# Attention with the product with v turned round, and ten chunks of inner features instead of nine in the first feed-forward phase

## The chip, the core and the metric

One core of a Trainium2 chip runs the whole program. The metric is the device time of one execution in microseconds (us); for the kernel before it is the median of three runs. An engine is named as the profile names it: PE is TensorE (matmuls), PEld its weight loads, DVE is VectorE, ACT is ScalarE, POOL is GpSimd, and SP is the queue that issues all DMAs here.

## What is computed

Causal attention with decay over 4 batches of 8 heads (576 positions, 64 features a head), a feed-forward layer of 2304 tokens (512 to 2048 to 512, leaky ReLU), and a second one (512 to 1024 to 512) with a softmax gate and a layer norm. Cut to what matters:

```python
scores = scale * np.matmul(q, k.transpose(0, 1, 3, 2))
scores = np.where(causal, -1000000000.0, scores + decay)
scores = scores - np.max(scores, axis=-1, keepdims=True)
attn = np.exp(scores)
attn = attn / (np.sum(attn, axis=-1, keepdims=True) + 1e-09)
return np.matmul(attn, v)                       # _attn_ref
h = x @ w_in; g = np.maximum(0.01 * h, h); return g @ w_out   # _moe_ref
solu = h * softmax(h); return layernorm(solu, g_ln) @ w_out   # _moe2_ref, shortened
```

## The kernel before

**How the order comes about.** The kernel doesn't write its instructions in the order in which they run. `body` declares operations (`P.op`) with an engine, an estimated duration, a priority and the buffers they write and read; `Plan.run` then plays them through a model of the engines and writes each instruction at the moment the model gives it an engine. A buffer is a tile of a tag (`P.tag("ps_v", ...)`); an operation whose tag has no free tile waits in the model, and a tile can be handed on to another tag when its own has no further use (`heirs`). On the chip each engine then runs its list strictly in that order. Attention has lower priority numbers (127 to about 500) than the feed-forward layer (from 1000), so feed-forward matmuls fill what attention leaves of PE.

**Attention** goes by pairs of heads: 16 pairs, four to a batch (`pair`, L765 on). The first four pairs are done in two parts, query blocks 0 and 1 (128 rows each) first and blocks 2, 3 and 4 later; the other twelve in one. For a unit of query blocks `scores` puts q times k into a PSUM bank `ps_s` (four banks), DVE adds the mask and takes the row's minimum (L693), and `softmax` goes on: ACT takes the exponential and sums the row (`accum_out`, L643), the sum is guarded and scaled (L652 to L657) and inverted (L661), ACT copies the row times the inverse to f16 as the high half (L424, tile `hl`), and DVE writes the rest as the low half (L435). A DMA turns `hl` into `pt` (L467), so that keys lie on the partitions. `pv` then multiplies: the stationary operand is a 128x128 block of v, 64 columns of high halves beside 64 of low halves (`vl`), and the moving one is `pt`, 128 queries wide:

```python
for k in range(2):
    mm(ps.t[:, 128 * i:128 * i + 128], vl(p, hd, j), pts[i][0].t[:, pts[i][1] + k * (i + 1) + j, :],
       j == 0 and k == 0, j == i and k == 1)
```

The result stands with features on the partitions, the high and the low sum in different halves, and `evac` adds the two and rescales (ACT L725, then DVE L728) into `xr`, which goes to memory. `pv4` does the same for block 4, whose 64 rows of both heads share one softmax; its moving operand is 64 wide. All products use the one PSUM bank `ps_v`.

**The feed-forward layer** goes in two phases over nine blocks of 256 tokens. In the first (`ffn_a`) `FA` = 9 of the 16 chunks of 128 inner features are computed for every block, and the partial output is stored; in the second (`ffn_b`) the other seven, then the second layer (`layer2`, `layer2_out`). A block of the first phase needs all four pairs of its batch in memory (`load_x`, `deps`): blocks 0 and 1 need batch 0, blocks 2 and 3 batch 1, blocks 4 and 5 batch 2, and blocks 6 to 8 batch 3. A chunk of one block takes 24 matmuls with 256 columns, so nine chunks take 216. The first phase starts when its weights have been unpacked from the staging tiles `wst` (`main`, L1024).

Of the kernel before, what the change touches and what calls it, by code (L numbers as in the profile page):

```python
# [24 lines left out]
FA = 9  # L25
PT = 4
NVT = 4
# [3 lines left out]
WI0 = 9  # L31
# [326 lines left out]
def body(tc, kqa, kq, vt, f, wa, w2i, w2o, gln, out):  # L358
# [16 lines left out]
    P.tag("raw", tiles(base, "raw", 2, [128, KQ], F32))  # L375
    P.tag("wk", tiles(base, "wk", 2, [128, 512], I32))
# [20 lines left out]
    mask = ap.tile([128, 512], BF16, name="mask")  # L397
    mask4 = ap.tile([128, S], BF16, name="mask4")
# [74 lines left out]
    def setup():  # L473
# [120 lines left out]
    def prep_v(p, prio):  # L594
# [6 lines left out]
        half = lambda l: v.t[:, :, :, l].rearrange("p j h d -> p (j h) d")  # L601

        def sums():
            with nc.allow_low_precision(reason="only the exponent of the largest sum is used"):
                nc.scalar.activation(v.t.rearrange("p j h l d -> p (j h l d)")[:, 0:640], R(), AF.Abs, accum_out=va.t)
# [6 lines left out]
            v.t.rearrange("p j h l d -> p (j h l d)")[:, 0:256].bitcast(F32), ps.t[:, 0:128], mask[:, 0:128], -1.0, -(2.0 ** -97),  # L612
            ALU.add, ALU.min, col(1)), prio + PV, w=[(vs, 1)], rw=[v], r=[ps])
# [3 lines left out]
        P.op(DVE, 70, lambda: nc.vector.tensor_scalar(u.t.bitcast(I32), e(), float(29 << 23), None, op0=ALU.subtract), prio + PV + 1,  # L617
# [18 lines left out]
    def softmax(parts, prio):  # L636


        sts, n, nb = parts[0][1], 0, len(parts)
        hl, pt = P.buf("hl"), P.buf("pt")  # L640
        one = parts[0][2] == parts[-1][2]
        for k, (view, _, j, W, pieces, ps) in enumerate(parts):
            P.op(ACT, act(W, 1, True) + 93, lambda view=view, j=j, k=k: nc.scalar.activation(  # L643
                view(), view(), AF.Exp, bias=sts.t[:, j:j + 1], scale=-1.0, accum_out=sts.t[:, 3 + k:4 + k]), prio,
                w=[(sts, 2)], rw=[ps], r=[(sts, j)])

        ns = 1 if one else nb
        total, scale = lambda: sts.t[:, 3:3 + ns], lambda: sts.t[:, 6:6 + ns]

        def guard(e):  # L650
            if one and nb == 2:
                nc.vector.scalar_tensor_tensor(scale(), total(), 1.0e-9, sts.t[:, 4:5], op0=ALU.add, op1=ALU.add)  # L652
                nc.vector.tensor_scalar(scale(), scale(), PS, None, op0=ALU.mult)
            elif e == ACT:
                nc.scalar.activation(scale(), total(), CP, scale=PS, bias=1.0e-9 * PS)
            else:
                (nc.vector if e == DVE else nc.gpsimd).tensor_scalar(scale(), total(), 1.0e-9, PS, op0=ALU.add, op1=ALU.mult)  # L657

        engs = (DVE,) if one and nb == 2 else REC_ENGS
        flex(engs, [{ACT: 100.0, DVE: 70.0 * nb, POOL: 165.0}[e] for e in engs], guard, prio, w=[(sts, 3)], r=[(sts, 2)])  # L660
        P.op(DVE, 75, lambda: nc.vector.reciprocal(sts.t[:, 9:9 + ns], scale()), prio, w=[(sts, 4)], r=[(sts, 3)])  # L661
        for view, _, j, W, pieces, ps in parts:
            rs = lambda j=j: sts.t[:, 9 + j:10 + j]
            for ho, lo, so, w in pieces:
                copy_f(lambda ho=ho, w=w: hl.t[:, ho:ho + w], lambda so=so, w=w, view=view: view()[:, so:so + w], w, prio,
                       engs=HI_ENGS, scale=rs, psum=True, w=[(hl, ho)], r=[ps, (sts, 4)])
            for ho, lo, so, w in pieces:
                sub_f(lambda lo=lo, w=w: hl.t[:, lo:lo + w], lambda so=so, w=w, view=view: view()[:, so:so + w],
                      lambda ho=ho, w=w: hl.t[:, ho:ho + w], w, prio, engs=(DVE,), scale=rs,
                      w=[(hl, lo)], r=[ps, (sts, 4), (hl, ho)])  # L670
                n += 2 * w
        turn(lambda: pt.t[:, 0:n // 128], lambda: hl.t[:, 0:n], n, prio - 500, w=[pt], r=[hl])
        return pt

    def scores(p, unit, hd, prio, full):

        sts, parts, n, at = P.buf("st"), [], 0, 0
        for j, i in enumerate(unit):
            W = 128 * (i + 1)
            joint = i < 2 and len(unit) > 1  # L680
            if i == 1 and joint:
                at = 128
            else:
                ps, at = P.buf("ps_s"), 0
            view = lambda at=at, W=W, ps=ps: ps.t[:, at:at + W]
# [3 lines left out]
                **({"rw": [ps]} if at else {"w": [ps]}))  # L689
            parts.append([view, sts, j, W, [(n, n + W, 0, W)], key, i])  # L690
            n += 2 * W
        for view, _, j, W, _, key, i in parts:
            P.op(DVE, dve(W) + 130, lambda i=i, j=j, view=view: nc.vector.tensor_tensor_reduce(  # L693
                view(), view(), mask[:, 384 - 128 * i:512], -0.125, 3.0e38, ALU.add, ALU.min, sts.t[:, j:j + 1]),
                prio, w=[(sts, j)], rw=[key])
        parts = [x[:6] for x in parts]
        pt = softmax(parts, prio)
        return {i: (pt, x[4][0][0] // 128) for i, x in zip(unit, parts)}

    def scores4(p, prio, full):  # L700
# [4 lines left out]
        for ps, k0, k1, init in ((pa, 0, 512, 3.0e38), (pb, 512, S, None)):  # L705
            def pe(ps=ps, k0=k0, k1=k1, Q=QK[p]):
                for hd in range(2):
# [5 lines left out]
                ps.t[:, 0:n], ps.t[:, 0:n], mask4[:, k0:k1], -0.125, sts.t[:, 1:2] if init is None else init,  # L713
# [412 lines left out]
```

## Time and profile before

| what | value |
|---|---|
| median of 3 runs | 850.28 us (850.12 to 850.7) |
| the profiled execution, its own time | 849.04 us |
| its span, first to last instruction | 847.2 us |
| PE busy | 777.7 us, 92% of the span |
| PEld busy | 707.1 us, 83% |
| DVE busy | 523.0 us, 62% |
| ACT busy | 488.8 us, 58% |
| POOL busy | 364.5 us, 43% |

The span and the time of one execution differ by 1.84 us that lie outside the first and last instruction. Busy shares are means over stages that differ: attention runs until 368 us, the first phase goes on alone until 464 us, and the second phase and second layer take the rest. A matmul's own duration holds its way through the array as well; what one costs in a row of its kind is the distance from one start to the next.

### The profile page before, as it was taken

The page shows a single profiled execution, that of the slowest core. Times are in us where ns is not written, and L with a number is a line of the kernel's source. Part 1 is how long each engine was busy: PE and PEld are TensorE (multiplying, and loading weights), DVE is VectorE, ACT ScalarE, POOL GpSimd, SP SyncE. Part 2 cuts the span into 40 slices and gives each one's busy share as a digit, 9 for nine tenths or more (in the row PEclk, how much of TensorE's full clock was granted, in tenths as well). Part 3 has the DMA queues.
Part 4 walks back from the last instruction along what each step waited for, and adds up shares of the span by engine and source line. Part 5 has one row for each costly group of instructions (what it writes and reads, how often), then busy time and mean ns, then how long its engine had stood idle before and what let it go on. Part 6 is the DMA issues. An engine that isn't in the chain of part 4 may idle for free.

```text
span 847.2 us, 15672 instructions
## 1 busy us (share of the span) xinstructions
PE 777.7 (92%) x5648; PEld 707.1 (83%) x5648; DVE 523.0 (62%) x1301; ACT 488.8 (58%) x1210; POOL 364.5 (43%) x433
## 2 busy tenths in 40 slices
PE   2477799987899999999999999999999999999997
PEld 2345689975798889999999998899889988998985
DVE  7899888887878788736544755334342434243641
ACT  5799798977988889736644533332433243324321
POOL 7888757546756474026311323322332233223321
PEclk9999899995899999999999999999999999999999
DMA  9799778787868786755554513321314131312113
GB/s 285 199 231 226 178 142 183 129 185 156 184 137 179 126 197 115 147 165 187 168 175 157 190 26 87 71 68 26 87 38 101 26 88 38 87 26 63 26 42 95
DMA packets 179757, 106.66 MB, mean 126 GB/s; under 512 B 146608, under 2 KB 162496, under 8 KB 179680
## 3 DMA queue, kind: packets, MB, share of 16 engines
q1 hardware_dynamic: 179680, 105.67, 52.3%
q8 instruction: 44, 0.72, 0.4%
q14 instruction: 33, 0.27, 0.1%
HBM read 55.72 MB, written 14.78 MB: 83 GB/s over the span
## 4 chain that ended last, share of the span: by engine, by line
PE 58%; DVE 4%; DMA 3%; ACT 3%; issue 1%; POOL 1%; DVEq 0%; SPq 0%; ACTq 0%; POOLq 0%
PE ps_f L470 36%; PE ph L470 11%; PE py L470 8%; DMA pt<-hl 2%; PE ps_s L470 1%; PE ps_v L470 1%; DMA tr<-hl 1%; ACT hl L424 1%; DVE hl L435 1%; DVE st L657 0%; ACT ps_s L643 0%; DVE g L841 0%; DVE raw L952 0%; DVE ps_s L693 0%; DVE s L944 0%
## 5 line engine op out<-in xcount | busy, mean ns | idle before, releaser
L470 PE MATMUL ps_f<-x,wi 128*128 128x256 f32 x972 | 129.6, 288 | 0.8 <-DVE g L841 0.8
L470 PEld LDWEIGHTS ps_f<-x,wi 128*128 128x128 f32 x972 | 123.6, 193 | 2.0 <-DVE g L841 1.2
L470 PE MATMUL ps_f<-g,wo 128*128 128x256 f32 x972 | 124.2, 283 | 1.2 <-DVE g L841 1.2
L470 PEld LDWEIGHTS ps_f<-g,wo 128*128 128x128 f32 x972 | 119.5, 188 | 1.8 <-DVE g L841 1.5
L470 PE MATMUL ps_s<-kq 128*128 128x512 f32 (+4 forms) x352 | 95.4, 396 | 25.8 <-DVE hl L435 22.4
L470 PE MATMUL ps_f<-x,wib 128*128 128x256 f32 x756 | 98.3, 281 | 0.7 <-DVE g L841 0.4
L470 PEld LDWEIGHTS ps_s<-kq 128*128 128x128 f32 x352 | 65.9, 226 | 39.2 <-DVE hl L435 22.2
L470 PE MATMUL ph<-wi,g 128*128 128x512 f32 x408 | 98.3, 396 | 0.0
L839 ACT ACTIVATE g<-ps_f 128x256 fp32r<-128x256 f32 x144 | 55.2, 383 | 71.9 <-PE ps_f L470 70.8
L470 PEld LDWEIGHTS ps_f<-x,wib 128*128 128x128 f32 x756 | 92.8, 188 | 1.8 <-DVE g L841 1.7
L470 PEld LDWEIGHTS ph<-wi,g 128*128 128x128 f32 x408 | 76.0, 188 | 17.6
L439 POOL TENSOR_TENSOR kq<-raw,kq 64x576 fp32r<-64x576 f32 (+2 forms) x55 | 82.6, 1502 | 14.6 <-ACT kq L424 9.2
L435 DVE SCALAR_TENSOR_TENSOR hl<-ps_s,st,hl 128x512 f16<-128x512 f32 (+4 forms) x160 | 82.2, 538 | 9.1 <-ACT hl L424 7.3
L643 ACT ACTIVATE ps_s<-ps_s,st 128x512 f32<-128x512 f32 (+4 forms) x160 | 78.8, 493 | 13.0 <-DVE st L693 7.7
L841 DVE TENSOR_TENSOR g<-ps_f,g 128x256 fp32r<-128x256 f32 x144 | 60.2, 420 | 41.0 <-ACT ps_f L840 39.3
L470 PE MATMUL ps_f<-wo,x 128*128 128x512 f32 x348 | 83.9, 396 | 0.0
L424 ACT ACTIVATE hl<-ps_s,st 128x512 f16<-128x512 f32 (+4 forms) x146 | 73.0, 538 | 12.3 <-issue 3.2
L470 PEld LDWEIGHTS ps_f<-wo,x 128*128 128x128 f32 x348 | 64.7, 188 | 14.9
L470 PE MATMUL ps_v<-pt,VT 128*128 128x128 f16 (+1 forms) x928 | 65.4, 234 | 12.7 <-DVE xr L728 4.3
L470 PE MATMUL py<-g,wob 128*128 128x256 f32 x567 | 76.6, 279 | 0.0
L470 PEld LDWEIGHTS <-VT 128*128 128x128 f16 x928 | 56.2, 110 | 22.8 <-issue 13.2
L470 PEld LDWEIGHTS py<-g,wob 128*128 128x128 f32 x567 | 72.4, 188 | 1.9
(152 smaller groups left out, 1198.5 us busy)
## 6 DMA issues: line engine op xcount, KB each, us to landing
wst<-wa SPq DMA_DIRECT2D x17, 512.0 KB
raw<-wa SPq DMA_DIRECT2D x15, 512.0 KB
raw<-kq SPq DMA_DIRECT2D x12, 608.0 KB
xw<-xs_d SPq DMA_DIRECT2D x24, 256.0 KB
yp_d<-yo SPq DMA_DIRECT2D x36, 128.0 KB
yw<-yp_d SPq DMA_DIRECT2D x18, 256.0 KB
out<-ot SPq DMA_DIRECT2D x18, 256.0 KB
vr<-vt SPq DMA_DIRECT2D x13, 320.0 KB
```

Source lines behind the costliest of these rows:

```text
L424: nc.scalar.activation(o, i, CP, scale=1.0 if scale is None else scale)
L435: nc.vector.scalar_tensor_tensor(o, a, scale, b, op0=ALU.mult, op1=ALU.subtract)
L439: (nc.vector if eng == DVE else nc.gpsimd).tensor_tensor(o, a, b, op=ALU.subtract)
L470: nc.tensor.matmul(o, lhsT=l, rhs=r, start=start, stop=stop)
L643: P.op(ACT, act(W, 1, True) + 93, lambda view=view, j=j, k=k: nc.scalar.activation(view(), view(), AF.Exp, bias=sts.t[:, j:j + 1], scale=- ...
L839: P.op(ACT, act(n, 0, True), lambda: nc.scalar.activation(g.t[:, 0, 0:n], h(), AF.Prelu, scale=WSC, alpha=0.01), eprio, w=[(g, 0)], r=[ps])
L841: P.op(DVE, dve(n) + 60, lambda: nc.vector.tensor_tensor(g.t[:, 1, 0:n], h(), g.t[:, 0, 0:n].bitcast(F32), op=ALU.subtract), eprio, w=[(g, ...
```

## The change

The product with v is turned round. `pt` is now the stationary operand (128 keys by 128 queries) and v the moving one: 65 columns of high halves, the 65th being ones, and 64 of low halves. So a query has a row, its 64 features beside each other, and the 65th column holds the sum of its weights. For one block of keys there are four matmuls (`pv_mms`) where there were two. `softmax` no longer sums, guards, inverts or rescales: it takes the exponential and splits it with a constant factor, and blocks 0 and 1 of a unit are split in one go. After the product three DVE operations (`divide`) guard the sums, invert them and scale the rows into `xn` (or `xn4`); PE turns these 128x128 blocks in its transpose mode (`across`, and the end of `pv4`) into `ps_v`, and one copy brings them to `xr`.

`FA` goes from 9 to 10, so a block of the first phase has 240 matmuls and one of the second 144 instead of 168. For the space, tiles `sd` are handed on as `xw` and `yo`, `x` has seven tiles instead of eight, and `yo` three instead of four. Cut to its core:

```diff
-FA = 9
+FA = 10
+NXN = 1
-WI0 = 9
+WI0 = 10
...
+        for v in P.tags["VT"].free:
+            nc.gpsimd.memset(v[:, 640:1300].rearrange("p (a d) -> p a d", d=66)[:, :, 64:65], 1.0)
...
-                view(), view(), AF.Exp, bias=sts.t[:, j:j + 1], scale=-1.0, accum_out=sts.t[:, 3 + k:4 + k]), prio,
+                view(), view(), AF.Exp, bias=sts.t[:, j:j + 1], scale=-1.0), prio, rw=[ps], r=[(sts, j)])
...
-        P.op(DVE, 75, lambda: nc.vector.reciprocal(sts.t[:, 9:9 + ns], scale()), prio, w=[(sts, 4)], r=[(sts, 3)])
...
+        for view, at, W, ps in groups:
+            copy_f(lambda at=at, W=W: hl.t[:, at:at + W], view, W, prio, engs=HI_ENGS, scale=lambda: 1.0 / PS, psum=True, w=[(hl, at)], r=ps)
+            sub_f(lambda at=at, W=W: hl.t[:, at + W:at + 2 * W], view, lambda at=at, W=W: hl.t[:, at:at + W], W, prio, engs=(DVE,),
+                  scale=lambda: 1.0 / PS, w=[(hl, at + W)], r=ps + [(hl, at)])
...
-    def evac(p, hd, ps, xr, c0, c1, dst0, prio):
...
+    def pv_mms(o, pair, v, first, last):
+        h, l = pair
+        vlo, vhi = v
+        mm(o, h, vhi, first, False)
+        mm(o[:, 0:64], h, vlo, False, False)
+        if l is not None:
+            mm(o[:, 0:64], l, vlo, False, False)
+            mm(o, l, vhi, False, last)
...
+    def divide(p, ps, rs, xn, dst, rows, nb, prio, key):
+        o = lambda a, b: ps.t[0:rows, 0:65 * nb].rearrange("p (n d) -> p n d", d=65)[:, :, a:b]
+        P.op(DVE, 70, lambda: nc.vector.tensor_scalar(rs.t[0:rows, 0:nb].unsqueeze(2), o(64, 65), 1.0e-9 / PS, None, op0=ALU.add), prio,
+             w=[(rs, 0)], r=[ps])
+        P.op(DVE, 75, lambda: nc.vector.reciprocal(rs.t[0:rows, 4:4 + nb], rs.t[0:rows, 0:nb]), prio, w=[(rs, 1)], r=[(rs, 0)])
+        P.op(DVE, dve(64 * nb) + 60, lambda: nc.vector.scalar_tensor_tensor(
+            dst(), o(0, 64), U[p].t[0:rows], rs.t[0:rows, 4:4 + nb].unsqueeze(2).to_broadcast([rows, nb, 64]),
+            op0=ALU.mult, op1=ALU.mult), prio, w=[(xn, key)], r=[ps, (rs, 1), U[p]])
...
+                    pv_mms(o, (pt.t[:, j, c], pt.t[:, 4 + j, c]), vl(p, hd, j), j == 0, False)
...
+        P.op(PE, 40.0, lambda: nc.tensor.transpose(ps.t[:, 256:320], xn.t.rearrange("p h d -> p (h d)"), ident[0:64, 0:64].bitcast(F32)), prio,
+             rw=[ps], r=[xn])
+        copy_f(lambda: xr.t[:, 512:S], lambda: ps.t[:, 256:320], 64, prio, engs=HI_ENGS, psum=True, w=[(xr, 1)], r=[ps])
+
+    def across(p, xn, blocks, xr, prio):
...
+            for i in blocks:
+                nc.tensor.transpose(ps.t[:, at(i)], xn.t[:, i], ident.bitcast(F32))
...
+        copy_f(lambda: xr.t[:, a:b], lambda: ps.t[:, a:b], b - a, prio, engs=HI_ENGS, psum=True, w=[(xr, 0)], r=[ps])
...
-        heirs("x", *(["x2"] * 4 + ["ln"] * 4))
+        heirs("x", *(["x2"] * 3 + ["ln"] * 4))
```

**What the order makes of it.** On PE, in the products of one head's query blocks with v. Before, each 128-column matmul has a weight load of v (`VT`) ahead of it:

```order
L470 LDWEIGHTS VT_108
L470 MATMUL ps_v_164<-pt_131,VT_108 128x128
L470 LDWEIGHTS VT_108
L470 MATMUL ps_v_164<-pt_131,VT_108 128x128
L470 LDWEIGHTS VT_108
L470 MATMUL ps_v_164<-pt_131,VT_108 128x128
```

Now each matmul of 65 or 64 columns has a load of `pt`, and there are twice as many of both:

```order
L477 LDWEIGHTS pt_135
L477 MATMUL ps_v_171<-VT_110,pt_135 128x65
L477 LDWEIGHTS pt_135
L477 MATMUL ps_v_171<-VT_110,pt_135 128x64
L477 LDWEIGHTS pt_135
L477 MATMUL ps_v_171<-VT_110,pt_135 128x64
L477 LDWEIGHTS pt_135
L477 MATMUL ps_v_171<-VT_110,pt_135 128x65
```

On DVE, after the product of block 4 in the changed kernel: the guard (L742) and the inverse (L744) of the sums, and a few rows later the scaling (L745) into `xn4`, between mask rows (`ISA`, L684), feed-forward rows (L858) and low halves (L442) of other units:

```order
L742 TENSOR_SCALAR rs_115<-ps_v_171 64x2
L744 RECIPROCAL rs_115<-rs_115 64x2
L684 ISA ps_s_168,st_126<-ps_s_168,mask 128x512
L684 ISA st_126 128x1
L858 TENSOR_TENSOR g_944<-ps_f_163,g_944 128x256
L745 SCALAR_TENSOR_TENSOR xn_118<-ps_v_171,u_119,rs_115 64x128
L442 SCALAR_TENSOR_TENSOR hl_133<-ps_s_169,hl_133 128x512
```

These rows take the place of the two halves of `evac`, and PE's turn of `xn4` waits for the sixth of them. On PE again, where blocks 0 and 1 of the first phase are used up and block 2 may begin. Before, these are the last rows of a stretch of 165 matmuls of attention without a feed-forward row in it, in which six groups of products with v lie:

```order
L470 MATMUL ps_s_161<-kq_0_140 128x512
L470 MATMUL ps_s_161<-kq_1_141 128x512
L470 MATMUL ps_s_162<-kq_0_144 128x64
L470 MATMUL ps_s_162<-kq_1_145 128x64
L470 MATMUL ps_s_162<-kq_0_140 128x64
L470 MATMUL ps_s_162<-kq_1_141 128x64
L470 MATMUL ps_f_154<-x_854,wi_63 128x256 x3
```

Now the stretch has 140 matmuls, with three groups of products in it, and ends with a turn:

```order
L477 MATMUL ps_s_169<-kq_0_147 128x384
L477 MATMUL ps_s_169<-kq_1_148 128x384
L477 MATMUL ps_s_170<-kq_0_149 128x512
L477 MATMUL ps_s_170<-kq_1_150 128x512
L775 MATMUL ps_v_171<-ident,xn_114 128x128 x4
L477 MATMUL ps_f_163<-x_936,wi_63 128x256 x3
```

Ahead of PE's last product with v stood 1188 matmuls of the first phase, and now 1020 stand ahead of its last turn.

## Rows read from the trace of the kernel before

**Rows 1.** The page's 40 slices: PE's busy tenths, and its granted clock.
```profile
PE   2477799987899999999999999999999999999997
...
PEclk9999899995899999999999999999999999999999
```
**Rows 2.** Busy time by stage: stretch and its length, each engine's busy us, clock, DMA share.
```profile
core 0: us, PE busy (x) PEld busy (x) DVE busy (x) ACT busy (x) POOL busy (x), PEclk, DMA share, GB/s
...
28.00:98.00 70.00, 45.67 (x246) 33.68 (x245) 63.76 (x178) 58.92 (x139) 56.44 (x62) 0.99 0.88 213
98.00:183.00 85.00, 82.52 (x744) 79.12 (x744) 71.14 (x223) 76.39 (x207) 52.06 (x50) 0.96 0.78 159
183.00:219.00 36.00, 24.52 (x168) 20.46 (x168) 29.87 (x91) 26.55 (x71) 21.30 (x22) 0.68 0.79 168
219.00:368.00 149.00, 143.90 (x1342) 137.08 (x1342) 118.32 (x360) 127.69 (x357) 71.39 (x76) 0.98 0.74 148
...
464.00:801.00 337.00, 336.33 (x2167) 303.60 (x2166) 151.60 (x290) 118.38 (x259) 99.55 (x147) 1.00 0.27 66
```
**Rows 3.** Groups of PE's matmuls by line between 98 and 183 us.
```profile
L470 PE MATMUL ps_f<-x,wi 128*128 128x256 f32 x216 | 31.1, 298 | 0.7 <-DVE g L841 0.7
L470 PE MATMUL ps_f<-g,wo 128*128 128x256 f32 x215 | 28.1, 284 | 1.2 <-DVE g L841 1.2
```
**Rows 4.** PE in order of time around the gap: start, us, instructions, idle before.
```profile
183.19 1.29 PE L470 MATMUL ps_v<-pt,VT 128*128 128x128 f16 x20
...
219.05 2.91 PE L470 MATMUL ps_f<-x,wi 128*128 128x256 f32 x12
```
**Rows 5.** Who waited for whom on PE: 28 to 98, 183 to 219, the whole run.
```profile
PE ps_s L470 <- DVE hl L435: 12.8, 9, 3.9
...
PE ps_s L470 <- DVE hl L435: 8.6, 3, 3.8
...
PE ps_v L470 <- DVE xr L728: 4.3, 4, 1.8
```
**Rows 6.** PE in order of time near attention's end.
```profile
361.80 0.70 PE L470 MATMUL ps_v<-pt,VT 128*128 128x64 f16 x18
362.34 4.56 PE L470 MATMUL ps_f<-x,wi 128*128 128x256 f32 x36
366.74 1.29 PE L470 MATMUL ps_v<-pt,VT 128*128 128x128 f16 x20
367.84 2.40 PE L470 MATMUL ps_f<-g,wo 128*128 128x256 f32 x18
```
**Rows 7.** PE in order of time, small f32 matmuls of the scores, and what follows them.
```profile
234.59 0.42 PE L470 MATMUL ps_s<-kq 128*128 128x128 f32 x2
234.84 1.65 PE L470 MATMUL ps_f<-x,wi 128*128 128x256 f32 x12
...
242.78 0.53 PE L470 MATMUL ps_s<-kq 128*128 128x64 f32 x4
243.14 1.68 PE L470 MATMUL ps_f<-g,wo 128*128 128x256 f32 x12
```
**Rows 8.** The chain that ended last: PE runs in the first phase and in the second.
```profile
368.03 13.02 PE ps_f L470 x108
...
464.95 1.76 PE ps_f L470 x15
```
**Rows 9.** The page's groups by line of what the softmax and `evac` lose.
```profile
L728 DVE SCALAR_TENSOR_TENSOR xr<-ps_v,u,xr 64x64 f32<-64x64 f32 (+2 forms) x72 | 34.7, 482 | 8.3 <-ACT xr L725 7.0
L725 ACT ACTIVATE xr<-ps_v,u 64x64 f32<-64x64 f32 (+2 forms) x72 | 33.8, 470 | 10.5 <-PE ps_v L470 6.4 <-DVE xr L728 2.7
L643 ACT ACTIVATION_READ_ACCUMULATOR ps_s<-ps_s,st 128x1 f32 x160 | 32.4, 203 | 0.2
L661 DVE RECIPROCAL st<-st 128x1 f32<-128x1 f32 (+2 forms) x88 | 14.2, 163 | 10.5 <-POOL st L657 6.7 <-ACT st L655 2.4
L652 DVE SCALAR_TENSOR_TENSOR st<-st 128x1 f32<-128x1 f32 x16 | 10.3, 642 | 0.5 <-ACT ps_s L643 0.3
```

More of the change, by code (lines that the diff above doesn't have):

```diff
@@ L375, in body @@
     P.tag("raw", tiles(base, "raw", 2, [128, KQ], F32))
+    P.tag("sd", tiles(base, "sd", 3, [128, S + 2], F32))
     P.tag("wk", tiles(base, "wk", 2, [128, 512], I32))
@@ L396, in body @@
     P.tag("va", tiles(ap, "va", 2, [128, 1], F32R))
[L397 to L398 removed]
+    mask = ap.tile([128, 640], BF16, name="mask")
+    mask4 = ap.tile([128, 64], BF16, name="mask4")
     zcol = ap.tile([32, 1], F32, name="zcol")
@@ L634, in qk_mm, with softmax @@
         mm(o, b[0:68, c0:c0 + 128], b[0:68, k0:k1], False, last)
-    def softmax(parts, prio):
-        sts, n, nb = parts[0][1], 0, len(parts)
+    def softmax(sts, parts, groups, prio):
         hl, pt = P.buf("hl"), P.buf("pt")
-        one = parts[0][2] == parts[-1][2]
-        for k, (view, _, j, W, pieces, ps) in enumerate(parts):
-            P.op(ACT, act(W, 1, True) + 93, lambda view=view, j=j, k=k: nc.scalar.activation(
-                view(), view(), AF.Exp, bias=sts.t[:, j:j + 1], scale=-1.0, accum_out=sts.t[:, 3 + k:4 + k]), prio,
[L645 to L660, printed above, removed]
-        P.op(DVE, 75, lambda: nc.vector.reciprocal(sts.t[:, 9:9 + ns], scale()), prio, w=[(sts, 4)], r=[(sts, 3)])
[L662 to L671, printed above, removed]
@@ L675, in scores @@
     def scores(p, unit, hd, prio, full):
-        sts, parts, n, at = P.buf("st"), [], 0, 0
+        sts, parts, groups, chunk, at = P.buf("st"), [], [], {}, 0
         for j, i in enumerate(unit):
@@ new lines, in pv_mms, with pv, pe @@
+    def pv_mms(o, pair, v, first, last):
[6 more added lines that the diff above has]
+            mm(o, l, vhi, False, last)
+    def pv(p, hd, pts, xn, prio):
+        ps, rs, blocks = P.buf("ps_v"), P.buf("rs"), sorted(pts)
+        bufs = {id(x[0]): x[0] for x in pts.values()}
+        nb, b0 = len(blocks), blocks[0]
+        def pe():
+            for n, i in enumerate(blocks):
+                pt, h, l = pts[i]
+                for j in range(i + 1):
+                    pv_mms(ps.t[:, 65 * n:65 * n + 65], (pt.t[:, h + j], pt.t[:, l + j]), vl(p, hd, j), j == 0, j == i)
+        P.op(PE, sum(4 * (i + 1) * mmh(65) for i in blocks), pe, prio, w=[ps], r=[VT[p]] + list(bufs.values()))
+        divide(p, ps, rs, xn, lambda: xn.t[:, b0 % 4:b0 % 4 + nb, 64 * hd:64 * hd + 64], 128, nb, prio, hd)
@@ L740, in pe @@
+    def across(p, xn, blocks, xr, prio):
+        ps = P.buf("ps_v")
+        at = lambda i: slice(128 * i, 128 * i + 128)
         def pe():
             for i in blocks:
-                for j in range(i + 1):
-                    for k in range(2):
-                        mm(ps.t[:, 128 * i:128 * i + 128], vl(p, hd, j), pts[i][0].t[:, pts[i][1] + k * (i + 1) + j, :],
-                           j == 0 and k == 0, j == i and k == 1)
-        P.op(PE, sum(2 * (i + 1) * mmh(128) for i in blocks), pe, prio, w=[ps], r=[VT[p]] + list(bufs.values()))
@@ L782, in pair @@
                 k += 1
+        across(p, xn, [i for i in blocks if i < 4], xr, prio + AV)
         c0, c1 = 128 * blocks[0], min(S, 128 * blocks[-1] + 128)
```

109 lines of the change are left out of this document (53 added, 56 removed).

## The prediction

> **What bounds the kernel now.** Read the slices of the page first [rows 1]: PE is nearly full from the middle on, and not in the first four slices or around the ninth and tenth, where its granted clock falls too. Then the table by stage [rows 2], which says why. From 464 to 801 us PE is busy 336.33 of 337 us; whatever the change adds to PE there, or takes, is paid in full. From 219 to 368 us, with attention and the first phase side by side, it is busy 143.90 of 149 us, and from 98 to 183 us 82.52 of 85 us. Two stretches are not PE's. From 28 to 98 us no feed-forward block is ready and attention runs alone: DVE is busy 63.76 of 70 us, the DMA engines 88%, PE 45.67 us. And from 183 to 219 us PE has nothing but attention again: it is busy 24.52 of 36 us at a mean granted clock of 0.68.
>
> The reason for that gap is the input of the first phase. Between 98 and 183 us PE ran 216 and 215 matmuls of it [rows 3], two blocks of 216 but for a record that is missing; the third needs batch 1. The time line shows no matmul of the first phase from 183.19 to 219.05 us [rows 4], and the waits in it are for a bank of scores that DVE has yet to free, 8.6 us in 3 waits, as from 28 to 98 us, 12.8 us in 9 [rows 5]. So the time is PE's work, plus what PE loses in these two stretches and at both ends. The change adds to the first and takes from the second.
>
> **What PE gets more of.** Prices are distances from one start to the next. Twenty products with 128 columns take from 366.74 to 367.84 us, 55 ns each; eighteen with 64 columns from 361.80 to 362.34 us, 30 ns each [rows 6]. Each has a weight load of its own, so the loads don't set the pace at either width.
>
> - Heads' blocks: 640 products of 55 ns (35.2 us) become 1280 of 64 or 65 columns at 30 ns (38.4 us): 3.2 us more.
> - Block 4: 288 of 30 ns (8.6 us) become 576 (17.3 us): 8.6 us more. Here the number doubles and the width stays.
> - Turns: 64 of 128 columns and 16 of 64, in f32. No row has one. The low end is the 55 ns of an f16 product of 128 columns [rows 6]; the high end twice the 125 ns at which two f32 matmuls of 128 columns stand (234.59 to 234.84 us), if a turn should need two passes. Four f32 matmuls of 64 columns in a row take 90 ns each (242.78 to 243.14 us) [rows 7]. Turns come in fours too, so I take 90 ns: 7.2 us (4.4 to 20).
> - The tenth chunk: 216 matmuls go from the second phase (15 in 1.76 us, 117.3 ns) to the first (108 in 13.02 us, 120.6 ns) [rows 8]: 0.7 us more.
>
> Together 19.7 us. What of it runs ahead of the first feed-forward row, where PE waits anyway, is free: by the changed order that is 280 products and 12 turns, 9.5 us, where the same units took 104 x 55 and 36 x 30 ns, 6.8 us. That leaves 19.7 - 2.7 = **17.0 us on the path**.
>
> The rows at 55 and 30 ns hold a load for every matmul. The Trainium skill ("TensorE: Matmul & The Clock Gate", Back-to-back issue gap) has a rule that speaks against the change: a stream of load and matmul pairs settles at about 81 ns for 128 columns, set by both. If a pair cost that at any width, 928 more pairs would be an estimated 75 us. The trace doesn't agree: 55 ns at 128 columns and 30 at 64.
>
> **What goes from the other engines.** ACT loses 160 reads of the sum (32.4 us) and 72 rows of `evac` (33.8 us), and gets 36 copies, at the 470 ns of an `evac` row 17 us. DVE loses 34.7, 14.2 and 10.3 us [rows 9] and gets 56 times guard, inverse and scaling; at 163, 163 and 482 ns from the same rows that is at most 45.2 us, so 14 us go at the least, of the 283 us that DVE is busy from 28 to 368 us [rows 2], or 5%. The scaled rows are shorter than most of `evac`'s, so it may be twice that. Where PE is full this hides behind PE and is worth nothing. It counts in the two other stretches:
>
> - **28 to 98 us.** DVE is 91% busy, so 5 to 10% of its work is 3 to 6 us. The DMA engines are 88% busy and have a weight chunk more to bring in here (`WI0` = 10), so 8.4 us is the most. I take 6 us.
> - **183 to 219 us.** Two blocks are now 480 matmuls of the first phase instead of 432, so they last 48 x 120.6 ns = 5.8 us longer, while attention, with a shorter chain in each unit, comes further beside them. The changed order has three groups of products in the gap where there were six. Half of 36 us is 18 us; the attention that has left it, half of 24.52 us at the lower level of 1.2 GHz, costs about 6 us elsewhere at 2.4 GHz: 12 us gained. In what is left a unit no longer waits for the sum's read (203 ns), the guard and the inverse (163 ns) [rows 9]; over three groups with some four units I take 2 us. Together 14 us.
>
> The handed-on tiles (`xw`, `yo`, seven `x`) I cost at nothing: the y matmuls of a block last 120 x 120.6 ns = 14.5 us, in which one more `x` tile has to be split. Where that cover fails, PE would wait at each block's start.
>
> **Sum.** 849.04 (the profiled execution) + 17.0 - 6 - 14 = 846.0 us, 3.0 us less. The median of the runs, 850.28 us, stands 1.24 us above that execution, so I forecast **847.2 us**, with a range of its own from 842 to 853. A measurement of this kernel can tell about 0.2%, or 1.7 us.
>
> **The rivals.**
>
> *The gap closes (faster).* If attention is held up by its chain more than I take, it reaches batch 1's end before the two blocks run out. For it: every wait in the gap is for a bank that the chain frees [rows 5], and the change takes pieces from just that chain. Against it: the order still has 140 matmuls there. The gap's full loss is 36 - 12.3 = 23.7 us, 9.7 more than I took, and the first stage may give its 8.4 us: 847.2 - 12.1 = 835 us.
>
> *Narrow weights (slower).* Block 4's stationary operand is now 64 columns wide, and no row has an f16 load of that width; the eighteen at 30 ns load 128. The nearest slow case is the f32 matmul of 64 columns at 90 ns with a 128-column load of f32 [rows 7], half of which, for half the columns, is 45 ns. Then 504 of the 576 products (72 stand in the first stage) cost 15 ns more each: 7.6 us, **854.8 us**. It decides from 36 ns a product on, where 504 x 6 ns eats the 3.0 us. The Trainium skill ("TensorE: Matmul & The Clock Gate", Weight-path perf modes) says that the fast load is used for 128 weights only, and gives a load of P columns as P / 1.2 ns, an estimated 53 ns here, or 11.6 us more; no row here shows it.
>
> *Turns that wait (slower).* PE stops in its order at a turn until three DVE rows are done, and feed-forward rows queue behind it. There are 36 such steps, 29 of them after the first feed-forward row. For it: PE waited for `evac`'s DVE row 4 times, 1.08 us each [rows 5]. Against it: 4 of 72. If one in three of the 29 waits that long, it is 10.4 us: 857.6 us.
>
> **How the numbers follow.** Forecast 0.40, gap closes 0.25, narrow weights 0.22, turns that wait 0.13. Of my own case half (0.20) ends under 848.6 us, 0.13 within 0.2%, and 0.07 above. So faster is 0.20 + 0.25 = 0.45, the same 0.13, slower 0.07 + 0.22 + 0.13 = 0.42. The range goes from 834, which takes in most of the closed gap, to 863, which takes in both slow rivals with turns at twice my price.
>
> **What would show it.** Right: 1,856 products at about 30 ns where PE runs full; turns near 90 ns; first matmul of the first phase at 90 to 94 us instead of 98; a gap of 14 to 18 us after 480 matmuls of it; attention's last turn about 20 us before 368 us (1020 instead of 1188 feed-forward matmuls stand ahead of it); no new wait of PE for `xn`. Wrong: block 4's products at 40 ns or more; a turn of 200 ns; PE's waits for DVE rows L745 summing to over 5 us; a gap as long as before, or none; or a second phase in which PE is less than 99% busy, for want of an `x` or `yo` tile.

## The result, and the profile after

The changed kernel takes 859.64 us (median of 4 runs, 859.17 to 866.02), the kernel before on the same chip 850.49 us (4 runs, 850.12 to 851.58): a ratio of 1.0123, 95% interval 1.0092 to 1.0153. It is slower, where 847.2 us was forecast. The profiled execution took 859.84 us, with a span of 858.0 us, 10.8 us more than before.

The page of the changed kernel, engines first, then the slices that answer to [rows 1]:

```profile
PE 791.4 (92%) x6656; PEld 720.9 (84%) x6656; DVE 471.9 (55%) x1212; ACT 438.0 (51%) x968; POOL 355.9 (41%) x414
...
PE   1756899999799899999999999999999899999997
...
PEclk9999999999999999999999999999999999999999
```

DVE and ACT got rid of 51 us each, and the dip of the clock in the tenth slice is gone. PE is busy 13.7 us longer. The table by stage, which answers to [rows 2] (PE's idle time is a stretch's length less its busy time):

```profile
core 0: us, PE busy (x) PEld busy (x) DVE busy (x) ACT busy (x) POOL busy (x), PEclk, DMA share, GB/s
0.00:100.36 100.36, 55.80 (x386) 43.30 (x386) 77.14 (x211) 66.81 (x129) 69.58 (x76) 1.00 0.87 223
28.00:100.36 72.36, 47.03 (x361) 36.34 (x359) 59.09 (x157) 50.44 (x99) 49.62 (x42) 1.00 0.85 210
...
211.40:223.90 12.50, 9.48 (x143) 8.39 (x141) 7.63 (x30) 7.81 (x17) 7.83 (x8) 0.86 0.47 113
...
480.00:808.00 328.00, 322.05 (x2061) 288.95 (x2060) 144.67 (x271) 119.45 (x253) 109.93 (x156) 1.00 0.30 76
...
100.36:480.00 379.64, 369.02 (x4008) 353.11 (x4007) 227.41 (x697) 237.79 (x561) 162.89 (x161) 0.99 0.64 148
```

The same stretches of the kernel before, cut at its own first matmul of the first phase and at 50 us ahead of its end:

```profile
0.00:98.08 98.08, 53.84 (x269) 39.82 (x270) 85.72 (x232) 77.82 (x183) 78.86 (x94) 1.00 0.87 228
...
480.00:797.20 317.20, 316.53 (x1997) 283.80 (x1996) 139.20 (x268) 108.72 (x237) 92.49 (x135) 1.00 0.26 62
...
98.08:480.00 381.92, 362.70 (x3179) 347.87 (x3180) 278.53 (x773) 288.40 (x766) 180.31 (x185) 0.96 0.70 161
```

The gap shrank from 35.9 to 12.5 us, more than forecast. The first phase starts at 100.36 us instead of 98.08, in spite of a DVE that is only 82% busy from 28 us on. And from 480 us on PE, which idled 0.67 us, now idles 5.95. What PE did at the lower of its two clock levels is in the stretches with a granted clock of 0.50, of before:

```profile
97.23:104.06 6.83, 6.83 (x29) 6.64 (x30) 5.63 (x17) 5.60 (x14) 6.68 (x7) 0.50 0.71 166
189.39:192.80 3.41, 3.41 (x24) 3.01 (x25) 1.97 (x8) 2.19 (x6) 2.60 (x2) 0.50 1.11 277
196.22:213.29 17.07, 13.78 (x82) 11.53 (x83) 13.66 (x44) 12.66 (x34) 10.49 (x11) 0.50 0.64 142
216.70:223.52 6.82, 6.82 (x37) 6.36 (x38) 4.57 (x16) 6.09 (x19) 5.56 (x8) 0.50 1.02 227
```

and of the changed kernel:

```profile
219.20:222.61 3.41, 3.33 (x43) 3.27 (x43) 0.88 (x5) 0.92 (x4) 0.61 (x1) 0.50 0.32 77
297.71:301.12 3.41, 3.41 (x17) 3.41 (x17) 3.02 (x8) 2.52 (x7) 3.34 (x3) 0.50 0.87 175
```

30.84 us of work at the lower level (1.2 instead of 2.4 GHz) became 6.74 us. What the level costs is seen at the first phase's start in the kernel before, where twelve feed-forward matmuls take 2.71 us, 226 ns each, against the 120.6 ns of [rows 8]:

```profile
98.08 2.91 PE L470 MATMUL ps_f<-x,wi 128*128 128x256 f32 x12
100.79 1.70 PE L470 MATMUL ps_s<-kq 128*128 128x512 f32 x4
```

So about half of the difference, an estimated 12.0 us, is time won between these two executions. It is a loose term: experiment 7, which has the same order on PE, spends 13.7 us at the lower level after the start of its first phase, and among the four runs of the changed kernel the profiled one has the highest mean granted clock (0.996; the others 0.986 to 0.992).

A granted clock of 1.00 isn't always the pace at which PE goes. Ahead of the first phase the page prints 1.00, yet the last 28 products there take 1.57 us in the changed kernel, 56 ns each. Forty in the stretch printed as 0.50 take 2.16 us, 54 ns each:

```profile
96.81 1.75 PE L477 MATMUL ps_v<-VT,pt 128*128 128x65 f16 x28
98.38 2.14 PE L477 MATMUL ps_s<-kq 128*128 128x384 f32 x6
...
219.28 2.35 PE L477 MATMUL ps_v<-VT,pt 128*128 128x65 f16 x40 [1.34 <-ACT xr L431]
221.44 1.59 PE L477 MATMUL ps_s<-kq 128*128 128x384 f32 x4
```

In experiment 8, with the same order on PE up to there, the same 28 take 0.85 us, 30 ns each:

```profile
93.12 1.02 PE L477 MATMUL ps_v<-VT,pt 128*128 128x65 f16 x28
93.97 1.54 PE L477 MATMUL ps_s<-kq 128*128 128x384 f32 x6
```

So a busy microsecond ahead of the start can be worth half of a later one, and the start depends on when PE's pace rises. The prices of what was added stand in PE's time line near attention's end, as in [rows 6]:

```profile
341.02 1.38 PE L477 MATMUL ps_v<-VT,pt 128*128 128x65 f16 x40
342.24 2.03 PE L477 MATMUL ps_f<-g,wo 128*128 128x256 f32 x15
344.20 1.33 PE L477 MATMUL ps_v<-VT,pt 128*64 128x65 f16 x36
345.45 3.14 PE L477 MATMUL ps_f<-x,wi 128*128 128x256 f32 x24
348.53 0.27 PE L764 MATMUL ps_v<-ident,xn 64*128 64x64 f32 x1
348.73 1.69 PE L477 MATMUL ps_f<-x,wi 128*128 128x256 f32 x12
...
354.44 0.60 PE L775 MATMUL ps_v<-ident,xn 128*128 128x128 f32 x4
354.79 1.44 PE L477 MATMUL ps_f<-x,wi 128*128 128x256 f32 x10
```

Forty products of a head take 1.22 us, 30.5 ns each; the 36 of block 4 take 1.25 us, 34.7 ns; four turns 0.35 us, 88 ns; a 64x64 turn 0.20 us. So the changed kernel asks of PE 1280 x 30.5 ns - 35.2 = 3.8 us for heads, 576 x 34.7 ns - 8.6 = 11.4 us for block 4, 64 x 88 + 16 x 200 ns = 8.8 us for turns and 0.7 us for the tenth chunk: 24.7 us. From these rows the balance is

| term | forecast, us | measured, us |
|---|---|---|
| PE's added work | +19.7 | +24.7 |
| of it free ahead of the first phase | -2.7 | 0 |
| PE idle ahead of the first phase | -6 | +0.3 (44.24 to 44.56) |
| gap and around it: lower clock level | part of -14 | -12.0 |
| gap and around it: PE idle from the first phase's start to 480 us | part of -14 | -8.6 (19.22 to 10.62) |
| PE idle from 480 us on | 0 | +5.3 (0.67 to 5.95) |
| sum | -3.0 | +9.7 (the span: +10.8) |

The 1.1 us between the sum and the span are not accounted for; the first line prices every product at the later pace, also those ahead of the first phase.

### The profile page after: what moved, and what is told of

Same layout as the page of the kernel before. It is cut to its first block, busy times and chain, and to the rows that moved or that the text cites. A ratio compares the mean times of both kernels' runs of the same rounds, so it can differ in the third digit from the quotient of the medians.

```text
span 858.0 us, 17359 instructions
## 1 busy us (share of the span) xinstructions
PE 791.4 (92%) x6656; PEld 720.9 (84%) x6656; DVE 471.9 (55%) x1212; ACT 438.0 (51%) x968; POOL 355.9 (41%) x414
## 4 chain that ended last, share of the span: by engine, by line
PE 71%; DMA 11%; DVE 7%; ACT 4%; issue 3%; POOL 3%; SPq 1%; POOLq 0%; DVEq 0%; ACTq 0%
PE ps_f L477 41%; PE ph L477 11%; PE ps_s L477 7%; PE ps_v L477 6%; PE py L477 5%; DMA sd<-xs_d 3%; DMA tr<-hl 2%; DMA wst<-wa 2%; DMA raw<-wa 2%; DMA pt<-hl 1%; DVE wst L815 1%; DVE kq L446 1%; DMA raw<-w2o 1%; SPq L468 1%; PE ps_v L775 1%
## 5 line engine op out<-in xcount | busy, mean ns | idle before, releaser
L477 PE MATMUL ps_f<-g,wo 128*128 128x256 f32 x1080 | 136.3, 283 | 0.0
L477 PEld LDWEIGHTS ps_f<-g,wo 128*128 128x128 f32 x1080 | 131.9, 188 | 0.3
L858 DVE TENSOR_TENSOR g<-ps_f,g 128x256 fp32r<-128x256 f32 x144 | 60.1, 420 | 60.3 <-ACT ps_f L857 57.6
L477 PEld LDWEIGHTS <-pt 128*128 128x128 f16 (+1 forms) x1856 | 69.0, 109 | 22.3 <-issue 18.9
L477 PE MATMUL ps_v<-VT,pt 128*128 128x65 f16 (+3 forms) x1856 | 74.7, 203 | 10.8 <-ACT xr L431 5.9
L477 PE MATMUL ps_f<-x,wib 128*128 128x256 f32 x648 | 82.8, 279 | 0.0
L477 PEld LDWEIGHTS ps_f<-x,wib 128*128 128x128 f32 x648 | 78.4, 188 | 0.1
L442 DVE SCALAR_TENSOR_TENSOR hl<-ps_s,hl 128x384 f16<-128x384 f32 (+2 forms) x128 | 69.6, 557 | 13.5 <-ACT hl L431 13.0
L684 DVE CUSTOM_DVE_ANT_0 ps_s<-ps_s,mask 128x128 f32<-128x128 f32 (+3 forms) x128 | 61.9, 498 | 21.8 <-PE ps_s L477 15.3
L477 PE MATMUL py<-g,wob 128*128 128x256 f32 x486 | 64.3, 277 | 0.0
L431 ACT ACTIVATE hl<-ps_s 128x384 f16<-128x384 f32 (+2 forms) x121 | 59.5, 512 | 9.1 <-DMA pt<-hl 8.3
```

The lines of the kernel that those rows point to most:

```text
L431: nc.scalar.activation(o, i, CP, scale=1.0 if scale is None else scale)
L442: nc.vector.scalar_tensor_tensor(o, a, scale, b, op0=ALU.mult, op1=ALU.subtract)
L477: nc.tensor.matmul(o, lhsT=l, rhs=r, start=start, stop=stop)
L858: P.op(DVE, dve(n) + 60, lambda: nc.vector.tensor_tensor(g.t[:, 1, 0:n], h(), g.t[:, 0, 0:n].bitcast(F32), op=ALU.subtract), eprio, w=[(g, ...
```

## The experiments

The theory when they began (A): PE's added work is paid in full, the gap gave more than forecast, the first stage gave nothing and the second phase lost. The rivals put the loss on the tenth chunk, on PE's waits at the turns, or on missing tiles. Ratios are to the kernel before on the same chip, with the 95% interval in brackets.

**1. The product alone, nine chunks.**

```diff
-FA = 10
+FA = 9
...
-WI0 = 10
+WI0 = 9
```

> The changed kernel with nine chunks in the first phase again (FA = 9, WI0 = 9): the turned product alone. Theory A (the added work of PE, about 24 us, is paid in full, and the gap around 200 us gives back about 12 us of it by attention's shorter chain and 6 us by the tenth chunk): two blocks end 48 x 120.6 ns = 5.8 us earlier, so the gap is 16 to 20 us long; the second phase is 99% busy again (5 us back); first matmul of the first phase at 98 to 101 us; together within 3 us of the changed kernel's 859.6. Rival B (the tenth chunk is what went wrong, in the first stage and in the second phase): 853 us or less, with the first matmul at 96 us or before.

Measured: 1.0163 [1.0143, 1.0184], no faster than the whole change (1.0123 [1.0092, 1.0153]; the intervals overlap). The gap is 16.6 us, as A had it. So the turned product costs as much by itself, and the time of rival B falls. But A was not right throughout: the first matmul of the first phase stands at 95.90 us, where A had 98 to 101 and B 96 or before, and PE idles 4.9 us from 480 us on here too, with nine chunks, which A had put down to the tenth.

**2. The tenth chunk alone**, the kernel before with the same constants and the tiles handed on.

```diff
-FA = 9
+FA = 10
...
-WI0 = 9
+WI0 = 10
...
+    P.tag("sd", tiles(base, "sd", 3, [128, S + 2], F32))
...
-            P.tag("x", tiles(mp, "x", 8, [128, 2, TB], F32R))
...
+            P.tag("x", tiles(mp, "x", 7, [128, 2, TB], F32R))
...
-            P.tag("yo", tiles(mp, "yo", 4, [128, TB], F32))
+            P.tag("yo", tiles(mp, "yo", 1, [128, TB], F32))
...
```

> The kernel before with ten chunks in the first phase, ten of them staged, and the tiles handed on (xw and yo on sd, seven x): the other half of the change alone. Theory A: the gap is 5.8 us shorter (30 us instead of 35.9), the second phase loses 5 to 6 us for want of x or yo tiles, the first matmul of the first phase stands at 98 to 99 us: 850 to 852 us, no difference from before. Rival B (the tenth chunk is what went wrong): first matmul at 100 us or later and 855 us or more. If neither loss appears, 844 us.

Measured: 1.0083 [1.0064, 1.0101]; the first matmul at 92.66 us, a gap of 32.4 us. It is slower by itself, and not as either theory had it: the first phase starts 5.4 us earlier than before. Its rows ahead of the first phase, from attention's end to 480 us, and from there on:

```profile
0.00:92.66 92.66, 47.07 (x240) 34.78 (x240) 78.98 (x212) 69.98 (x162) 72.24 (x85) 0.94 0.90 232
376.95:480.00 103.05, 98.50 (x812) 97.47 (x812) 41.35 (x73) 46.61 (x115) 25.00 (x31) 1.00 0.43 136
480.00:806.60 326.60, 320.10 (x2033) 286.50 (x2032) 143.42 (x268) 117.50 (x251) 108.74 (x156) 0.99 0.28 74
```

PE idles 4.6 and 6.5 us in the last two, where the kernel before idles less than 1 us in all; the gap gave back 3.5. And the early start shows no gain: PE had idled 45.6 us by then, where it idles 44.2 us before, and had done 240 matmuls instead of 269.

**3. Nine of the ten chunks staged early.**

```diff
-WI0 = 10
+WI0 = 9
```

> The changed kernel, with the tenth chunk's weights brought in after the first stage (WI0 = 9, FA still 10). Theory A (the first stage is held by DVE, and by PE standing in its order at turns): first matmul of the first phase still at 100 us, time 858 to 860. Rival (the eighteenth staged chunk holds the first block's weights or the queue): first matmul at 98 us or before, 856 to 857.5 us.

Measured: 1.013 [1.0115, 1.0146], and the first matmul at 93.71 us. The first phase starts 6.7 us earlier, as the rival said, but nothing of it shows in the time. One row tells a part of why:

```profile
0.00:93.71 93.71, 49.41 (x348) 37.51 (x349) 74.32 (x201) 65.41 (x125) 67.62 (x75) 0.98 0.87 224
```

Idle by then: 44.3 us, against 44.56 us in the changed kernel. PE had run 38 matmuls fewer, and been busy 6.4 us less. Over the fourteen kernels of this study the first phase starts between 92.66 and 100.36 us, and PE has idled 41.6 to 45.6 us by then. The start itself is loose: the changed kernel and experiments 7, 8 and 9 have the same order on PE through the whole first phase, and start it at 100.36, 97.86, 95.35 and 96.09 us, with 43.6 to 45.6 us idle. Of the 5.0 us between the changed kernel and experiment 8, 1.8 are there at PE's first matmul (17.67 and 15.88 us), and 2.7 come about behind 80 us, where PE's pace rises in experiment 8 and not yet in the changed kernel. So neither the later start of the changed kernel (100.36 against 98.08 us) nor the earlier one here can be put down to a change in the code, and whether the eighteenth staged chunk delays it isn't shown.

**4. Guard, inverse and scaling first on DVE.**

```diff
     def divide(p, ps, rs, xn, dst, rows, nb, prio, key):
+        prio = prio - 500.0
```

> The changed kernel with guard, inverse and scaling of the sums, and the turns behind them, put 500 priority units ahead of other DVE work, so that PE stands less at a turn. Theory A' (PE's 18.5 us of waits for xn before 100 us delay the stage): these waits fall under 9 us, the first matmul of the first phase comes at 94 to 97 us, 854 to 857 us. Rival (DVE's own work sets that stage, the waits are slack of PE): the waits fall, the first matmul stays at 99 to 101 us, 858 to 861 us.

Measured: 1.0100 [1.0077, 1.0122], against 1.0123 [1.0092, 1.0153]: the right direction, but the intervals overlap. The waits ahead of the first phase stayed, 17.8 us in the profiled execution:

```profile
PE ps_v L776 <- DVE xn L746: 7.3, 4, 4.6
PE ps_v L477 <- DVE xn L746: 5.4, 2, 5.1
PE ps_v L765 <- DVE xn L746: 5.1, 1, 5.1
```

The first matmul came at 94.97 us all the same, and PE had idled 41.6 us. The edit didn't do what it was meant to do: the waits that it was to halve are still there, so it tests neither the theory nor the rival. The start came as the theory had it, but it is as loose as experiment 3 says.

**5. A product left out.** The low half of the weights times the low half of v is not computed: three matmuls for a block of keys instead of four. The planned durations go down with it, so the order is written anew.

```diff
-            mm(o[:, 0:64], l, vlo, False, False)
```

> The changed kernel without the product of the weights' low half with v's low half (left out: one of the four products for a block of keys, 464 of 1,856 matmuls). Theory A (PE's products are paid in full wherever they stand): 464 x 30 to 35 ns = 14 to 16 us, of which the 70 ahead of the first feed-forward matmul (2 us) fall in waits, so 12 to 14 us less than the changed kernel, 846 to 848 us, and PE busy 14 us or more shorter. Rival (attention's chain or the tiles hold the time, PE's products lie in its waits): less than 6 us gained, 854 us or more, with the waits of PE longer instead.

Measured: 847.47 us, 0.9968 [0.9947, 0.999], some 13 us less than the changed kernel. Its page:

```profile
PE 778.1 (92%) x6208; PEld 708.7 (84%) x6208; DVE 466.8 (55%) x1205; ACT 441.9 (52%) x976; POOL 356.1 (42%) x413
```

448 matmuls (464 were expected) and 13.3 us of PE gone, 30 ns each, and about as much of the time (some runs of this kernel differ by 10 us, 842.89 to 852.53, but the interval leaves no doubt of the sign). PE's work is paid in full, within what this can tell, although the gap is 18.8 us here instead of 12.5; the rival falls.

**6. The product alone with as many tiles as before**, on top of experiment 1. With nine chunks there is room for them.

```diff
-            P.tag("x", tiles(mp, "x", 7, [128, 2, TB], F32R))
+            P.tag("x", tiles(mp, "x", 8, [128, 2, TB], F32R))
...
-            P.tag("yo", tiles(mp, "yo", 1, [128, TB], F32))
+            P.tag("yo", tiles(mp, "yo", 2, [128, TB], F32))
...
-        heirs("x", *(["x2"] * 3 + ["ln"] * 4))
+        heirs("x", *(["x2"] * 4 + ["ln"] * 4))
```

> The turned product alone with nine chunks, as in the run of that name, but with as many x and yo tiles as the kernel before has (x eight, four of them handed on to the second phase, yo four). Theory T (the missing tiles made PE's waits after attention's end, 9.9 us in that run from 344 to 809 us): these waits fall under 2 us and the time to 1.005 to 1.009 of the kernel before. Rival (those waits come from DVE and POOL being late, whatever the tiles): the waits stay at 8 us or more, and the ratio at 1.013 or above.

Measured: 1.0081 [1.006, 1.0101], 0.8% less than experiment 1. The second phase of experiment 1, and then of this one:

```profile
480.00:809.10 329.10, 324.20 (x2062) 290.33 (x2062) 143.21 (x269) 114.37 (x249) 99.10 (x147) 0.99 0.26 65
```

```profile
480.00:804.30 324.30, 323.51 (x2085) 290.42 (x2084) 146.40 (x280) 115.55 (x252) 93.63 (x137) 1.00 0.26 67
```

4.9 us of idle time became 0.8. With nine chunks the second phase lost for want of tiles, and the ratio is the one that theory T had. Its number for the waits is missed: from attention's end to 480 us PE still idles 4.8 us, with one wait of 3.5 us for a split row in it.

**7. The same tiles in the second phase of the changed kernel.** Ten chunks leave it room.

```diff
-            P.tag("x2", tiles(bp, "x2", 2, [128, 2, TB], F32R))
+            P.tag("x2", tiles(bp, "x2", 3, [128, 2, TB], F32R))
+            P.tag("yo", tiles(bp, "yob", 1, [128, TB], F32))
```

> The changed kernel with one x2 tile and one yo tile more in the second phase alone, where ten chunks leave room for them (six and four then, as before). Theory T: PE's idle time from 480 to 808 us falls from 5.95 us to under 1.5 us and the ratio to the kernel before from 1.012 to 1.006 to 1.008. Rival (fewer rows of PE a block as cover, 144 instead of 168 matmuls ahead of a block's second layer, are the cause): idle time stays above 4 us and the ratio at 1.011 or above.

Measured: 1.0117 [1.0081, 1.0152], PE idle 5.8 us from 480 us on. With ten chunks theory T falls. One of the waits of PE there, 1.25 of the 5.95 us, can be followed in the changed kernel. DVE in order of time:

```profile
577.67 0.41 DVE L858 TENSOR_TENSOR g<-ps_f,g 128x256 fp32r<-128x256 f32 x1
587.77 0.43 DVE L434 CAST x<-tr 128x512 fp32r<-128x512 f16 x1 [9.69 <-DMA tr<-hl]
588.12 0.42 DVE L858 TENSOR_TENSOR g<-ps_f,g 128x256 fp32r<-128x256 f32 x1
```

and PE:

```profile
588.68 1.64 PE L477 MATMUL ps_f<-wo,x 128*128 128x512 f32 x6 [1.25 <-DVE g L858]
```

DVE stands for 9.69 us at a cast of the second layer, whose tile a DMA is still turning, and the row of a feed-forward bank that PE needs stands behind it in DVE's order. DVE's waits for that DMA from 480 to 800 us, before and then after:

```profile
DVE x L427 <- DMA tr<-hl: 12.9, 3, 7.8
```

```profile
DVE x L434 <- DMA tr<-hl: 43.3, 6, 10.9
```

In experiment 7 itself they are 21.9 us, half, and PE idles as long. So these waits of DVE don't by themselves set PE's idle time.

**8 and 9. Two other orders for the second phase**, on top of experiment 7: the rows that empty the y banks first, and an order written as if that DMA took 3 us more.

```diff
-                y32.t, at[d](), WSC * WSC, yw.t[:, d % 2], op0=ALU.mult, op1=ALU.add), eprio + 20, w=[y32], r=[py[d], yw])
+                y32.t, at[d](), WSC * WSC, yw.t[:, d % 2], op0=ALU.mult, op1=ALU.add), eprio - 4000, w=[y32], r=[py[d], yw])
```

> The run with more second-phase tiles, and the DVE rows that empty the y banks (L934) put ahead of the second layer's DVE rows. Theory O (with 144 matmuls a block the order that was written puts y rows behind second-layer rows, which wait for POOL or for the DMA turn of the second layer): PE's waits for L934, 4.0 us there after 355 us, go to nothing, and its idle time from 480 to 808 us falls from 5.57 to about 3 us, what is left being waits for L858. Rival (DVE simply has too much work in a block of 144): waits move from L934 to L858 and the idle time stays at 5 us or more.

```diff
-        return P.op(SP, max(350.0 + 0.875 * n, 1175.0), lambda: nc.sync.dma_start_transpose(out=dst(), in_=src()), prio, dma=0.875 * n, **kw)
+        return P.op(SP, max(350.0 + 0.875 * n, 1175.0), lambda: nc.sync.dma_start_transpose(out=dst(), in_=src()), prio, dma=0.875 * n + (3000.0 if n == 2048 else 0.0), **kw)
```

> The run with more second-phase tiles, where the order is now written as if the second layer's DMA turn took 3 us more; nothing else is changed, and nothing before the second phase. Theory O: DVE no longer stands for up to 10.9 us at casts of the turned tile (L434) with split rows of the hidden features (L858) behind it, so its waits for that DMA fall from 21.9 us to under 8 and PE's idle time from 480 to 808 us from 5.57 to under 3 us: 3 us or more off the ratio of 1.012. Rival (too much work in a block): idle time above 4.5 us and the same time.

Measured: 1.0119 [1.0099, 1.0138] and 1.014 [1.0122, 1.0158]. In the first the waits for L934 are gone and PE idles 3.9 us instead of 5.8; in the second DVE's waits for the DMA fell to 6.8 us, but PE still idles 5.5 us, 3.9 of it at L858. Neither made the kernel faster. So order moves these waits about, and which part of them ten chunks make unavoidable is open.

**10 and 11. Nine chunks, the tiles of before, and no low-low product**: the edits of experiments 1, 6 and 5 together, and then that of experiment 4 as well.

> The turned product alone, nine chunks and as many x and yo tiles as before (ratio 1.0081), without the low half of the weights times the low half of v (464 of 1,856 products left out). Theory A: PE's products are paid in full here too: 13 us less, a ratio of 0.992 to 0.995, and PE busy 777 us. Rival (with nine chunks the time is held by the chain in the gap): 0.998 or above.

> As the run before it, with guard, inverse and scaling of the sums 500 priority units earlier. With ten chunks that took the ratio from 1.0123 to 1.0100. Theory A': 1 to 3 us less than without it, 0.990 to 0.993. Rival: PE's waits for those rows are slack, no difference within 0.2%.

Measured: 845.95 us, 0.9966 [0.9953, 0.9979], and 844.33 us, 0.9943 [0.992, 0.9966]. The first is 1.15% under the product alone with all four matmuls (expected 1.3 to 1.6%), and no better than experiment 5 with ten chunks (0.9968): with less work beside it the gap grew from 16.8 to 23.8 us. Its ratio lies between the range of A and that of the rival. The second is faster than both kernels of this case, but both leave out a product that these compute. That "divide first" gave 0.2% both times makes a small gain likely; each of the two pairs of intervals overlaps.

**12. Ten chunks once more**, on experiment 11, with the edits of 7 and 8.

> The run before it (nine chunks, without the low-low product, divide first; ratio 0.9943, gap of 21.8 us, PE idle 0.5 us from 480 us to 50 us before the end) with ten chunks instead, and with what mended most of the second phase at ten chunks (x2 six, yo four, y rows first). Theory C (the tenth chunk takes its 5.8 us from the gap and gives back about as much in the second phase, whatever the tiles): the gap is 15 to 18 us long, PE idle 3 to 5 us in the second phase, and the ratio 0.991 to 0.997, no difference from nine chunks. Rival (with the second phase mended the tenth chunk pays): idle under 2 us and a ratio under 0.990.

Measured: 1.002 [1.0002, 1.0037], slower than with nine chunks. That is outside what either theory had. PE idles 3.2 us in the second phase, as theory C had it, but the gap didn't shrink: with nine chunks, and then with ten, it is

```profile
191.00:212.80 21.80, 15.63 (x163) 12.18 (x159) 14.45 (x57) 14.68 (x33) 15.39 (x17) 0.76 0.82 183
```

```profile
203.50:227.10 23.60, 15.32 (x157) 12.40 (x156) 17.03 (x52) 16.44 (x36) 13.45 (x13) 0.67 0.94 193
```

Two blocks end 12.5 us later, and attention needs 14.3 us longer to come to batch 1's end. Why the order gives it so little beside ten chunks is open. Where nine chunks had their tiles, the tenth paid in no pair of runs (1.0081 and 1.0123, 0.9966 and 0.9968, 0.9943 and 1.002). With as few tiles as ten chunks leave, nine came out higher (1.0163 and 1.0123), with intervals that overlap.

## Why the prediction was wrong, point by point

- **The bound (PE's work plus what PE loses in two stretches)** was right, and experiments 5 and 10 show it: 448 products fewer, 13.3 us of PE, took 13 and some 10 us off.
- **Prices.** The heads' products (30 ns forecast, 30.5 measured) and the 128-column turns (90 and 88) were right. *Narrow weights* decided from 36 ns and came to 34.7: a part of that rival is true, 2.8 us. The Trainium skill ("TensorE: Matmul & The Clock Gate", LDWEIGHTS (loading the stationary operand), the section ahead of the one that the prediction names) would have had a load of 64 columns last an estimated 53 ns; the rows don't agree, with 34.7 ns for load and product. I missed the 64x64 turns, which stand alone between feed-forward matmuls and take 0.20 us: 1.8 us more than at 90 ns. Together with the heads' 0.6 us the added work was undersized by 5.0 us.
- **"What of it runs ahead of the first feed-forward row ... is free" and "28 to 98 us ... I take 6 us" failed.** The first phase was to start at 90 to 94 us, with the added work ahead of it hidden in PE's waits. In the four kernels with this order it starts at 95.35 to 100.36 us, and PE has idled 43.6 to 45.6 us by then, where it idles 44.24 before: no 6 us came out of the stage. Nor did the added work go into the waits: PE's busy time ahead of the start rose from 53.84 to 55.80 us. (Idle time in one order spreads over 2 us, so 0.3 us is no difference. And neither it nor the start alone measures the stage, since PE's pace there differs from run to run.) That DVE fell from 91% to 82% busy [rows 2] took no idle time from PE, which now stands in its order behind the turns:

```profile
PE ps_v L775 <- DVE xn L745: 9.1, 3, 4.0
PE ps_s L477 <- DVE hl L442: 5.4, 5, 2.3
PE ps_v L764 <- DVE xn L745: 4.8, 2, 4.4
PE ps_v L477 <- DVE xn L745: 4.6, 3, 3.2
```

  These waits of the changed kernel from 28 to 100.4 us stand against 12.8 us for `hl` before [rows 5]: the chain lost its guard and inverse ahead of the product and got them back behind it. That the waits at the turns are what holds the stage now is read from these rows; no run shows it, since experiment 4 left them at 17.8 us. *Turns that wait* named the mechanism, but for the wrong place: 18.5 us ahead of the first phase, 1.1 us in the gap. Two terms, 8.7 us, were credited for nothing.
- **The gap** was right in kind and undersized: 12.5 us long (14 to 18 forecast), and 20.6 us won in it and around it instead of 14. Of what is printed at the lower clock level most is gone, at the first phase's start (97.23 to 104.06 us) too, which I had not counted: the granted clock of [rows 1] has it as an 8 in the fifth slice, and its dip in the tenth and eleventh. And the waits for a bank of scores, 8.6 us, are not the whole of what PE idled in the gap, 11.5 us [rows 2]. *The gap closes* didn't happen.
- **"The handed-on tiles ... I cost at nothing" failed.** From 480 us on PE is 98.2% busy, not 99%. The cover that I named, one x tile beside 14.5 us of y matmuls, is not what failed: with nine chunks one x tile and one yo tile cost 4.1 us there and 0.8% of the time (experiment 6); with ten as much is lost with the tiles or without (experiment 7). The old product with ten chunks and few tiles loses it too, 6.5 us (experiment 2), so it does not hang on the turned product. One such wait, 1.25 us, comes from DVE standing at a DMA with a row behind it that PE needs, but an order with fewer of these waits lost as much elsewhere (experiment 9). What causes the rest with ten chunks is open.
- These steps in sum: 5.0 + 2.7 + 6.3 + 5.3 - 6.6 = 12.7 us, of the 13.8 us between the forecast for the profiled execution, 846.0 us, and its 859.84.

**What stays open:** what holds the stage ahead of the first phase, and when PE's pace rises in it; how much of the second phase's waits ten chunks force, and why the gap of experiment 12 is as long as that of 11.

## What to carry to other kernels

Where a stage ahead of a full engine is to get shorter, look at what that engine has idled and what it has done by the stage's end, and at which pace, and not at the end alone: work that is only moved across the border is not gained. Run one order more than once before a few microseconds of a start are put down to a change. Price an added matmul by its own width and its place, one that stands alone among others too. And a tile given up for space is a change to every stage that uses it: look for the engine whose list stands still, in order, at a transfer.

## What the runs showed of the hardware

An f16 matmul of 64 or 65 columns with a load of its own takes 30.5 ns with 128 weight columns and 34.7 ns with 64, so the narrower load was not the cheaper one. Ahead of the first phase the same product with 128 weight columns took 56 ns in one execution and 30 ns in another of the same order, both under a granted clock printed as 1.00. Four f32 turns of 128x128 in a row take 88 ns each, and one of 64x64 between feed-forward matmuls 0.20 us.
